# The cold start of a fused spectral-filter and feed-forward kernel: filters in three groups of loads, half of the forward table moved back, spare matmuls, a split last product

## The chip, the cores and the metric

One NeuronCore of one Trainium2 chip runs the whole program. The metric is device time in microseconds (us). Runs sent together share one chip and the same runs of the kernel before; runs sent at another time were on another chip, and I compare across those only through their ratios to the kernel before.

## The reference, cut to what matters

```python
X = np.fft.rfft(x, axis=1)                    # x: 8 batches, 3008 positions, 256 channels
F = (filt_r + 1j * filt_i)[None, :, :]
y = np.fft.irfft(X * F, n=3008, axis=1)       # then, with y as 24064 tokens of 256:
h = y @ w_in                                  # 256 -> 2048
out = (0.5 * h * (1.0 + erf(h / sqrt(2)))) @ w_out   # 2048 -> 256
```

## The kernel before

The Fourier transforms are matrix products with tables that the kernel computes itself. 3008 is factored as 47 x 64, which gives two forward steps (c1, c2), a product with the filters, and two backward steps (c3, c4), with transposes (c1t, c3t) between. Batches 1 to 7 are transformed beside the dense layers. **Batch 0 is not**: the dense layers cannot begin before it, so its whole chain stands in the open. That chain, and the tables and loads that it needs, are what the change rearranges. The parts concerned, with cuts:

```python
    def load_filters(self, k0, k):            # 4 loads on Pool's queue: real, imaginary, direct, mirror
        for t, src in enumerate((self.filt_r, self.filt_i)):
            ...
                nc.gpsimd.dma_start(out=self.F[32 * q:32 * q + 32, t, k0:k0 + k, :], in_=a)

    def dup_filters(self, eng, k0, k):        # partitions 0-63 copied to 64-127, two k at a time
        for k in range(k0, k0 + k, 2):
            o, i = (self.F[r:r + 64, :, k:k + 2, :].rearrange(...) for r in (64, 0))
            eng.tensor_copy(out=o, in_=i)

    def table_2_swap(self, h):                # half h of the forward table: rows swapped by PE, written by ACT
        t2 = self.T2[:, 12 * h:12 * h + 12]
        for s, j in ((1.0, 0), (-1.0, 32)):
            ps = self.bank("ps_sw", "n")
            self.nc.tensor.matmul(ps[:, 0:384], lhsT=self.swap, rhs=t2[:, :, 1, j:j + 32], ...)
            self._evac(t2[:, :, 2, j:j + 32], ps[:, 0:384].rearrange(...), "act", s)

    def table_2_minus(self, h):               # and its negative, by DVE
        self.nc.vector.tensor_scalar(out=t2[:, :, 0, :], in0=t2[:, :, 2, :], scalar1=-1.0, op0=ALU.mult, ...)
```

```python
    m.psum(wide, w=(2, 2), n=(4, 1))          # PSUM: two pairs of banks "w", four single banks "n"
    ...
    for k, n in ((0, 4), (4, 2), (6, 4), (10, 6), (16, 8)):
        m.load_filters(k, n)                  # 20 loads
    m.dup_filters(nc.gpsimd, 6, 4)
    m.load_w_in()
    ...
    m.dup_filters(nc.gpsimd, 10, 14)
    for u in range(16):
        m.c1(u // 2, u % 2, act if u < 4 or u % 2 else False)
        if u == 3:
            m.table_2_sin(0)
            m.table_2_swap(0)
        if u == 7:
            m.table_2_minus(0)
            m.table_2_sin(1)
            m.table_2_swap(1)
            m.table_2_minus(1)
        if u == 11:
            m.table_3(0, False)
    ...
    m.c1t(0, False)
    m.c1t(1, act)
    m.dup_filters(nc.vector, 0, 6)            # DVE copies the first six k itself
    for q in range(7):
        if q < 6:
            m.c2(2 * q)                       # products 2q and 2q+1: PE into a pair "w", DVE multiplies by F
            if q + 2 < 6:
                m.c1t(q + 2, act)
            m.c2(2 * q + 1)
        ...
        if q >= 1:
            m.c3(q - 1)
    ...
    m.psum(wide, v=(2, 2), t=(3, 1))
    for u in range(10):
        if u < 8:
            m.c3t(u)                          # transposes on PE, copied to d by DVE; u = 0 has a Pool memset of vt's end
        if u >= 2:
            m.c4(u - 2, False if u == 8 else act)   # both halves in one pair of banks, one evacuation
```

## Time and profile before

| before | us |
|---|---|
| time, median of 3 (later runs: 788.1 to 791.7) | 790.59 |
| span of the profiled run, whose time was 788.94 | 787.17 |
| first filter product starts | 22.54 |
| last filter product ends | 36.96 |
| first dense product starts | 46.67 |
| from there to the end | 740.50 |

The times inside the span are read from the timeline (start and duration of each row). The last row is PE-bound and untouched by the change.

### The profile page before, as it was taken

To read this page: it belongs to the slowest core of one execution; us is meant where nothing else is said; L and a number is where in the kernel's file an instruction comes from. 1 tells how busy PE (TensorE), PEld (TensorE's weight loads), DVE (VectorE), ACT (ScalarE), POOL (GpSimd) and SP (SyncE) were. 2 spreads that over 40 slices of the span, in tenths; PEclk is the share of its full clock that TensorE was granted. 3 is DMA by queue.
4 is the path that set the end of the run, shared out by engine and by line. 5 is a ranking of instruction groups with operands and counts; after the bars stand their busy time and mean duration, and the time that the engine had idled before them with its cause. 6 is when DMAs were issued, how large, how long until landed. Compare 5 with 4: busy or idle time off the path is not lost.

```text
span 787.2 us, 14592 instructions
## 1 busy us (share of the span) xinstructions
PE 762.2 (97%) x5821; PEld 540.1 (69%) x5918; DVE 406.7 (52%) x720; ACT 567.4 (72%) x968; POOL 65.7 (8%) x161
## 2 busy tenths in 40 slices
PE   4899999999999999999999999999999999999997
PEld 4766766677676767667677766667767677666666
DVE  6884756365563645546455564536645376411011
ACT  4788965788558975588755886568965788666663
POOL 8800200010000100001000110001100000000000
PEclk9999999999999999999999999999999999999999
DMA  8874753465334652447614465164642521510111
GB/s 130 151 135 139 140 148 79 144 123 113 106 101 141 115 146 74 108 131 139 146 40 123 138 126 149 49 172 92 130 121 73 157 80 56 134 37 32 41 41 55
DMA packets 86469, 85.64 MB, mean 109 GB/s; under 512 B 5888, under 2 KB 76608, under 8 KB 86400
## 3 DMA queue, kind: packets, MB, share of 16 engines
q1 hardware_dynamic: 77760, 68.70, 31.0%
q0 software_dynamic: 8640, 16.00, 14.3%
q8 instruction: 46, 0.75, 0.4%
q14 instruction: 23, 0.19, 0.1%
HBM read 54.00 MB, written 46.66 MB: 128 GB/s over the span
## 4 chain that ended last, share of the span: by engine, by line
PE 93%; DMA 3%; issue 1%; POOL 1%; ACT 1%; DVE 1%; SPq 0%; DVEq 0%; POOLq 0%
PE ps_o L450 42%; PE ps_h L436 38%; PE ps_s L253 3%; PE ps_s L326 3%; PE ps_s L276 2%; PE ps_s L301 2%; DMA d_sb<-R 1%; DMA x_sb<-in_x_dram 1%; ACT y_sb L238 1%; PE ps_c L380 1%; POOL F L91 1%; PE ps_c L364 1%; DMA b_sb<-R 0%; POOL x_sb L82 0%; DMA F<-in_filt_i_dram 0%
## 5 line engine op out<-in xcount | busy, mean ns | idle before, releaser
L439 ACT ACTIVATE g_sb<-ps_h 128x512 bf16<-128x512 f32 x752 | 439.4, 597 | 189.0 <-PE ps_h L436 162.0
L450 PE MATMUL ps_o<-w_out_sb,g_sb 128*128 128x256 bf16 x3008 | 449.1, 272 | 3.0
L436 PE MATMUL ps_h<-y_sb,w_in_sb 128*128 128x512 bf16 (+2 forms) x1503 | 426.6, 365 | 0.7 <-ACT y_sb L238 0.7
L450 PEld LDWEIGHTS <-g_sb 128*128 128x128 bf16 x3008 | 287.6, 98 | 133.7
L436 PEld LDWEIGHTS <-w_in_sb 128*128 128x128 bf16 x1600 | 155.0, 98 | 23.4 <-issue 0.9
L454 DVE COPY ost<-ps_o 128x512 f32<-128x512 f32 x94 | 64.4, 685 | 125.2 <-PE ps_o L450 124.7
L284 DVE TENSOR_TENSOR p<-ps_s,F 128x512 bf16<-128x512 f32 x84 | 58.1, 692 | 104.2 <-ACT p L283 97.6
L242 DVE TENSOR_SCALAR y_sb<-ps_s 128x376 bf16<-128x376 f32 x112 | 61.0, 548 | 81.6 <-PE ps_s L326 81.6
L240 DVE CAST a_sb<-ps_s 96x512 bf16<-96x512 f32 x112 | 76.3, 685 | 41.3 <-PE ps_s L253 41.3
L240 DVE CAST v_sb<-ps_s 128x512 bf16<-128x512 f32 x84 | 57.6, 687 | 12.9 <-PE ps_s L301 12.3
L282 ACT ACTIVATE p<-ps_s 64x512 bf16<-64x512 f32 x84 | 49.9, 594 | 2.4 <-PE ps_s L276 0.3
L326 PEld LDWEIGHTS <-d_sb 96*128 96x128 bf16 x448 | 30.4, 97 | 27.9 <-DMA d_sb<-R 2.6
L283 ACT CAST p<-ps_s 64x512 bf16<-64x512 f32 x84 | 48.5, 577 | 1.0
L101 POOL COPY gate<-p 1x1 bf16<-1x1 bf16 x48 | 8.5, 176 | 483.7 <-DVE p L286 483.7
L253 PE MATMUL ps_s<-x_sb,T 94*96 94x512 bf16 x112 | 42.6, 381 | 0.5
L326 PE MATMUL ps_s<-T,d_sb 96*128 96x94 bf16 x448 | 36.5, 204 | 2.0 <-DMA d_sb<-R 0.6
L286 DVE TENSOR_TENSOR p<-p 128x512 bf16<-128x512 bf16 x84 | 35.7, 425 | 2.9
L285 DVE TENSOR_TENSOR p<-p,F 128x512 bf16<-128x512 bf16 x84 | 34.9, 416 | 0.0
L82 POOL DMA_DIRECT2D x_sb<-in_x_dram x64 | 32.5, 510 | 13.3 <-issue 11.2
L276 PE MATMUL ps_s<-b_sb,T 128*128 128x256 bf16 x168 | 32.1, 273 | 0.8 <-DMA b_sb<-R 0.5
L301 PE MATMUL ps_s<-p,T 128*128 128x256 bf16 x168 | 32.1, 273 | 0.2
L301 PEld LDWEIGHTS <-T 128*128 128x128 bf16 x168 | 16.4, 98 | 20.1 <-DVE p L286 0.5
(94 smaller groups left out, 192.8 us busy)
## 6 DMA issues: line engine op xcount, KB each, us to landing
out_dram<-ost SPq DMA_DIRECT2D x94, 256.0 KB, 2.5
x_sb<-in_x_dram POOLq DMA_DIRECT2D x64, 188.0 KB, 3.9
R<-a_sb SPq DMA_DIRECT2D x56, 192.0 KB, 3.0
b_sb<-R SPq DMA_DIRECT2D x28, 384.0 KB, 4.3
R<-v_sb SPq DMA_DIRECT2D x42, 256.0 KB, 3.9
d_sb<-R SPq DMA_DIRECT2D x56, 192.0 KB, 4.7
w_in_sb<-in_moe_w_in_dram POOLq DMA_DIRECT2D x2, 512.0 KB, 6.3
w_out_sb<-in_moe_w_out_dram POOLq DMA_DIRECT2D x2, 512.0 KB, 10.7
```

What stands on the lines that cost most here:

```text
L240: self.nc.vector.tensor_copy(out=out, in_=in_)
L242: self.nc.vector.tensor_scalar(out=out, in0=in_, scalar1=scale, scalar2=None, op0=ALU.mult)
L253: nc.tensor.matmul(ps[0:96, :], lhsT=self.T1, rhs=self.st[b, "x"][:, 2 * u:2 * u + 2, :], start=True, stop=True)
L282: nc.scalar.activation(out=p2[0:64], in_=ps[64:128], func=AF.Copy, scale=-1.0)
L283: nc.scalar.copy(out=p2[64:128], in_=ps[0:64])
L284: nc.vector.tensor_tensor(out=p1, in0=ps, in1=f(0), op=ALU.mult)
L301: nc.tensor.matmul(ps[:, 256 * i:256 * i + 256], lhsT=self.T3[:, k].rearrange("p a b -> p (a b)"), rhs=w[:, 256 * i:256 * i + 256], start= ...
L326: nc.tensor.matmul(ps[:, 94 * i:94 * i + 94], lhsT=d[:, (grp % 2) * 4 + i, 128 * half:128 * half + 128], rhs=t4, start=True, stop=True)
L436: nc.tensor.matmul(ps[:, o:o + n], lhsT=self.w_in_sb[:, dc, jc * 128:jc * 128 + 128], rhs=self.ring[:, dc, off:off + n], start=(dc == 0), ...
L439: nc.scalar.activation(out=self.st["g", t][:, jc, :], in_=ps, func=AF.Gelu)
L450: nc.tensor.matmul(ps[:, tile_i % 2, :], lhsT=g[:, jc, tile_i * 128:tile_i * 128 + 128], rhs=self.w_out_sb[:, jc, :], start=(jc == 0), sto ...
L454: nc.vector.tensor_copy(out=ost, in_=ps)
```

## The change

The change means to bring the first dense product forward. It has five parts: (1) filters in three groups of loads (12 issues in place of 20), all copied by Pool; (2) the second half of the forward table (swap, minus), and table 3, moved from the middle of c1 to behind it, with the Gelu table load moved up; (3) the last product in two halves and c3 ordered by halves; (4) c3t ordered by halves, and c4 evacuated half by half out of five single banks; (5) ten spare matmuls while the input loads and three in c1, for PE's clock. The diff, with cuts (the new order of c3 is left out):

```diff
     def table_2_swap(self, h):
-        for s, j in ((1.0, 0), (-1.0, 32)):
-            ps = self.bank("ps_sw", "n")
-            ...
+        ps = self.bank("ps_sw", "w")
+        for i in range(2):
+            self.nc.tensor.matmul(ps[:, i, 0:384], lhsT=self.swap, rhs=t2[:, :, 1, 32 * i:32 * i + 32],
+                                  start=True, stop=True)
+        ...
+    def warm_up(self, n):
+        ps = self.bank("ps_warm", "n")
+        for i in range(n):
+            self.nc.tensor.matmul(ps, lhsT=self.ones[:, 0:128], rhs=self.ones, start=True, stop=True)
     def c2(self, p):
+        if p < 11:
+            nc.vector.tensor_tensor(out=w, in0=ps, in1=f.rearrange(...), op=ALU.mult)
+            return
+        for c in (slice(0, 128), slice(128, 256)):
+            nc.vector.tensor_tensor(out=w[:, :, :, c], in0=ps[:, :, :, c], in1=f[:, :, :, c], op=ALU.mult)
     def c3t(self, u):
-        for i in range(8):
+        for i in (0, 2, 4, 6, 1, 3, 5, 7):
     def c4(self, u, eng):
-        ps = self.bank("ps_c4", "v")
         for half in range(2):
+            ps = self.bank("ps_c4", "v")
             ...
-        self._evac(yv, ps[:, :, 0:376].rearrange(...), eng, 1.0 / self.S)
+            self._evac(yv, ps[:, 0:376].rearrange(...), eng[half], 1.0 / self.S)
 ...
+    m.ones = g.tile([128, 512], BF16, name="ones")
+    nc.vector.memset(m.ones, 1.0)
+    m.warm_up(10)
-    for k, n in ((0, 4), (4, 2), (6, 4), (10, 6), (16, 8)):
+    for k, n in ((0, 4), (4, 8), (12, 12)):
         m.load_filters(k, n)
-    m.dup_filters(nc.gpsimd, 6, 4)
     m.load_w_in()
-    m.dup_filters(nc.gpsimd, 10, 14)
+    m.dup_filters(nc.gpsimd, 0, K1)
     for u in range(16):
-        m.c1(u // 2, u % 2, act if u < 4 or u % 2 else False)
+        m.c1(u // 2, u % 2, act if u < 4 or u % 2 and u != 15 else False)
         if u == 3:
+            m.warm_up(3)
             m.table_2_sin(0)
+        if u == 7:
             m.table_2_swap(0)
-        if u == 7:
             m.table_2_minus(0)
+        if u == 11:
             m.table_2_sin(1)
-            m.table_2_swap(1)
-            m.table_2_minus(1)
-        if u == 11:
-            m.table_3(0, False)
+            nc.scalar.activation(out=warm, in_=m.p, func=AF.Gelu)
-    m.dup_filters(nc.vector, 0, 6)
     for q in range(7):
             m.c2(2 * q)
+            if q == 0:
+                m.table_2_swap(1)
             ...
-        if 1 <= q < 3:
+        if q == 1:
+            m.table_2_minus(1)
+        if q < 3:
             m.table_3(q, act)
 ...
-    m.psum(wide, v=(2, 2), t=(3, 1))
+    m.psum(wide, v=(5, 1), t=(3, 1))
```

More of the change, by code (lines that the diff above doesn't have):

```diff
@@ L191, in table_2_swap @@
         t2 = self.T2[:, 12 * h:12 * h + 12]
-        for s, j in ((1.0, 0), (-1.0, 32)):
-            ps = self.bank("ps_sw", "n")
-            self.nc.tensor.matmul(ps[:, 0:384], lhsT=self.swap, rhs=t2[:, :, 1, j:j + 32], start=True, stop=True)
-            self._evac(t2[:, :, 2, j:j + 32], ps[:, 0:384].rearrange("p (k j) -> p k j", k=12), "act", s)
+        ps = self.bank("ps_sw", "w")
+        for i in range(2):
+            self.nc.tensor.matmul(ps[:, i, 0:384], lhsT=self.swap, rhs=t2[:, :, 1, 32 * i:32 * i + 32],
+                                  start=True, stop=True)
+        for i in range(2):
+            self._evac(t2[:, :, 2, 32 * i:32 * i + 32], ps[:, i, 0:384].rearrange("p (k j) -> p k j", k=12),
+                       "act", 1.0 - 2.0 * i)
     def table_2_minus(self, h):
@@ L366, in c2 @@
                                  rhs=self.st[0, "b", k // 4][:, k % 4, :], start=True, stop=True)
-        nc.vector.tensor_tensor(out=w, in0=ps, op=ALU.mult,
-                                in1=self.F[:, :, 2 * p:2 * p + 2, :].rearrange("p t a b -> p t (a b)"))
+        f = self.F[:, :, 2 * p:2 * p + 2, :]
+        if p < 11:
+            nc.vector.tensor_tensor(out=w, in0=ps, in1=f.rearrange("p t a b -> p t (a b)"), op=ALU.mult)
+            return
+        w, ps = (v.rearrange("p t (a b) -> p t a b", a=2) for v in (w, ps))
+        for c in (slice(0, 128), slice(128, 256)):
+            nc.vector.tensor_tensor(out=w[:, :, :, c], in0=ps[:, :, :, c], in1=f[:, :, :, c], op=ALU.mult)
     def c3(self, q):
@@ L374, in c3 @@
         ps = [self.bank("ps_c3", "n") for half in range(2)]
-        for i in range(4):
+        for i, half in ((0, 0), (1, 0), (0, 1), (1, 1), (2, 0), (3, 0), (2, 1), (3, 1)):
             w = self.st[0, "p", 2 * q + i // 2]
-            for half in range(2):
-                o = 256 * (i % 2) + 128 * half
-                for t in range(2):
-                    self.nc.tensor.matmul(ps[half][:, 128 * i:128 * i + 128], lhsT=w[:, t, o:o + 128],
-                                          rhs=self.T3[:, 4 * q + i].rearrange("p a b -> p (a b)"),
-                                          start=t == 0, stop=t == 1)
+            o = 256 * (i % 2) + 128 * half
+            for t in range(2):
+                self.nc.tensor.matmul(ps[half][:, 128 * i:128 * i + 128], lhsT=w[:, t, o:o + 128],
+                                      rhs=self.T3[:, 4 * q + i].rearrange("p a b -> p (a b)"),
+                                      start=t == 0, stop=t == 1)
         for half in range(2):
@@ L409, in c4 @@
         d = self.st[0, "d", u // 2]
-        ps = self.bank("ps_c4", "v")
         for half in range(2):
+            ps = self.bank("ps_c4", "v")
             for i in range(4):
-                self.nc.tensor.matmul(ps[:, half, 94 * i:94 * i + 94],
+                self.nc.tensor.matmul(ps[:, 94 * i:94 * i + 94],
                                       lhsT=d[:, 4 * (u % 2) + i, 128 * half:128 * half + 128],
                                       rhs=self.T4c.rearrange("p a b -> p (a b)"), start=True, stop=True)
-        yv = self.ring[:, :, 0:self.S].rearrange("c h (m w) -> c h m w", w=HB)[:, :, :, 4 * u:4 * u + 4]
-        self._evac(yv, ps[:, :, 0:376].rearrange("c h (i m) -> c h m i", i=4), eng, 1.0 / self.S)
+            yv = self.ring[:, half, 0:self.S].rearrange("c (m w) -> c m w", w=HB)[:, :, 4 * u:4 * u + 4]
+            self._evac(yv, ps[:, 0:376].rearrange("c (i m) -> c m i", i=4), eng[half], 1.0 / self.S)
     def segs(self, t):
@@ L535 @@
             m.c2(2 * q + 1)
-        if 1 <= q < 3:
+        if q == 1:
+            m.table_2_minus(1)
+        if q < 3:
             m.table_3(q, act)
-        if q == 3:
-            nc.scalar.activation(out=warm, in_=m.p, func=AF.Gelu)
         if q >= 1:
@@ L551 @@
         if u >= 2:
-            m.c4(u - 2, False if u == 8 else act)
+            m.c4(u - 2, (act, False if u > 7 else act))
     wide.close()
```

## The prediction

> **What bounds the kernel now.** I read the page first. PE is 97% busy over a 787.2 us span, and its row of slices is full from the second slice on; only the first slice has room (PE 4 tenths, POOL 8).
>
> ```profile
> span 787.2 us, 14592 instructions
> PE   4899999999999999999999999999999999999997
> DVE  6884756365563645546455564536645376411011
> POOL 8800200010000100001000110001100000000000
> ```
>
> So the body is bound by PE and nothing in the diff touches it: every changed line belongs to the start, in which batch 0 is transformed before the first product of the dense layers. That product (L436) starts at 46.67 us. The question is how far it moves; all behind it moves along. The chain of waits narrowed to the start, then the timeline, show how the 46.67 us come about:
>
> ```profile
> 12.32 4.60 POOL F L91 x9
> 16.92 2.73 DMA F<-in_filt_i_dram
> 19.73 1.33 DVE F L96 x2
> ...
> 22.10 0.42 DVE F L96
> ```
>
> ```profile
> 19.68 2.21 POOL L96 COPY F<-F 64x1024 bf16<-64x1024 bf16 x2
> 19.73 2.78 DVE L96 COPY F<-F 64x1024 bf16<-64x1024 bf16 x3
> 22.54 4.62 DVE L367 TENSOR_TENSOR p<-ps_c,F 128x1024 bf16<-128x1024 f32 x4
> 23.82 6.93 POOL L96 COPY F<-F 64x1024 bf16<-64x1024 bf16 x7
> 27.82 9.14 DVE L367 TENSOR_TENSOR p<-ps_c,F 128x1024 bf16<-128x1024 f32 x8 [0.66 <-POOL F L96]
> 37.79 0.69 DVE L240 CAST vt_sb<-ps_c 128x512 bf16<-128x512 f32 x1 [0.83 <-PE ps_c L380]
> 39.24 5.56 DVE L240 COPY d_sb<-ps_c3t 96x1024 bf16<-96x1024 bf16 x8 [0.75 <-PE ps_c3t L399]
> 40.52 4.72 ACT L238 ACTIVATE y_sb<-ps_c 128x752 bf16<-128x752 f32 x6 [2.25 <-DVE d_sb L240]
> 45.30 0.49 PE L413 MATMUL ps_c<-T4c,d_sb 96*128 96x94 bf16 x8 [0.29 <-ACT y_sb L238]
> 45.83 0.80 ACT L238 ACTIVATE y_sb<-ps_c 128x752 bf16<-128x752 f32 x1 [0.58 <-PE ps_c L413]
> 46.67 0.38 PE L436 MATMUL ps_h<-y_sb,w_in_sb 128*128 128x512 bf16 x1 [0.67 <-ACT y_sb L238]
> ```
>
> The columns are start, duration of the row, engine, line, operation, count. Three stages follow one another. (1) Until 22.54: tables, c1, c1t, loading of the filters and their copying to the upper partitions. (2) 22.54 to 36.96: twelve filter products on DVE, 1.14 us apart, hardly interrupted. (3) 36.96 to 46.67: c3t and c4, where PE, ACT and DVE alternate.
>
> **What the skill says.** "SBUF — State Buffer", section "SBUF: two separate sides": DVE and GpSimd share one port pair under an exclusive lock, taken by a DVE operation in a two-port mode; the loser waits out the whole instruction. The trace agrees: the first two DVE copies of F start at 19.73 and 20.92, beside Pool's, and together end at 22.17 (about 1.25 us each), while the third, after Pool's pair, is 0.42. The products, with one input from PSUM, aren't held: they keep their 1.14 us beside Pool's copies. "TensorE: Matmul & The Clock Gate", Part 1: the array runs at half rate until about 3.4 us of sustained work, and falls back after an idle window. The trace agrees on the two rates: four 256-column products take 0.89 us at 21.41 and 0.44 at 24.95 (the chain's figure); the trace's first record of the full clock is at 22.0. "ScalarE: Activation LUTs", section "What ACT_TABLE_LOAD costs": an ACTIVATE with immediate scale takes 186 ns + 0.833 ns per element, back-to-back ones overlap by 93 ns, and a table load costs 1283 ns. Here 128x384 takes 493 (506 by the formula), 128x752 797 (812), the table load 1283.
>
> **Part 1, the filters: the start of stage 2.** Before, 20 Pool issues of about 0.53 us end at 19.64, and only then do copies begin. From the landing times in the trace: each Pool issue waits for the DMA eight before it; the last x load lands at 12.38 and the first four filter loads (0 to 3 in k) at 12.70 to 13.72. Until 13.3 Pool is held by these landings and the change can't hurry it. Behind that 4 issues remain in place of 12: 13.32 + 4 x 0.52 = 15.4. The two w_in issues (1.32, plus the two small T1 copies: 1.9 in all, as at 21.84 to 23.76) end at 17.3. They need the 5th and 6th filter load, now 128 KB each; I put those at 14.5 and 15.3, from 0.75 us for 128 KB (four such landed in 3.04 us between 21.46 and 24.50), so there is no wait. First copy: 17.36 + 1.04 = 18.4, then one each 0.98 us. Products can follow at 18.45 instead of 22.54. Pool's 0.98 outpaces DVE's 1.14, so the later copies stay ahead. The last filters, 4 x 192 KB behind about 17, land at some 21.5; copy 7 wants them at 23.3.
>
> **Part 2, the tables: does c2 arrive by 18.45?** Moving swap, minus and table 3 (DVE 1.23 us at 15.72) behind c1 removes what delayed c1's evacuations. ACT gains the Gelu table load behind the second sine (1.28 + 0.2, taken away from q = 3), and the last c1 tile goes to DVE. By hand: u = 8 waits for DVE at 11.4 as before (its angle chain ends at 10.91, unchanged), ACT does u = 9 and 11 until 12.65, sine until 13.5, load and warm until 15.0, u = 13 until 15.4; c1t(0) 15.45 to 16.0, DVE copy 0.69, c2(0) done 17.4. That is 1.1 us of slack behind Pool; at the half clock 0.3. So **Pool sets the start: 4.1 us earlier.**
>
> **Part 3, costs inside stage 2.** (a) swap(1) takes one of the two "w" bank pairs between c2(0) and c2(1), so c2(1) must wait for product 0: 1.14 becomes 1.22 + 0.65 (the matmuls and their latency) once, +0.7. (b) minus(1) lands on DVE between products 3 and 4 in a two-port mode: 0.35 alone, up to 1.3 behind a Pool copy, +0.85. (c) The last product in halves: 2 x 0.69 instead of 1.14, +0.2. (d) Before, 0.66 was lost at product 4, which I don't count on: -0.66 in the time after. Products: 18.45, 20.4, 21.55, 22.7, then 24.7 and on to 34.0, against 36.96: the 4.1 have shrunk to 3.0. I checked every c1t, table 3 and c3 of ACT and PE against this; ACT has about 0.8 us of slack.
>
> **Part 4, the end.** The halves let c3's first half go early, but ACT first evacuates c3(4) and table 4 (until about 34.65), so vt's half is ready at 35.25, and DVE's at 35.1: c3t begins 1.3 after the last product, before 1.6 (36.96 to 38.54). With even transposes first, the first d copy starts 0.5 to 0.6 later in place of 0.7, and is done at 36.6 against 39.93: 3.3. From there before took 6.7: six ACT evacuations paced by PE at 0.785 (PE's 0.45 + 0.33 per u), then c4(7), held for ACT's bank until 45.30 and evacuated alone, 0.8. After: 14 ACT halves at an estimated 186 + 313 - 93 = 406 ns from the ScalarE page (0.38 apart on the 128x384 of c1 here), started 0.25 sooner as half a c4 suffices; five banks take away the wait; c4(7)'s halves go to two engines, 0.5 each. DVE's eight copies (5.5) and two halves (1.05) end about as late. That is 6.0: 0.7 less. **mm1 at 42.65 instead of 46.67: 4.0 us.**
>
> **Part 5, spare matmuls.** Ten of 128x512 at the half clock are 4.3 us, from about 1.0 to 5.3, while PE waits for x until 5.95: free. They matter only if the clock stays up. In c1 afterwards PE would be working less than half the time and stands still from 12.9 to 15.4. A fall back to half rate before 20 us would add some 0.45 to c2(1) and 0.6 to c2(2), both now on the path: 1.0. I give it one in two: -0.5. It leaves **3.5 us**, 790.6 - 3.5 = 787.1.
>
> **Rivals.** *DVE simply follows Pool.* If Pool's copies are stretched to 1.2 us (as one of them was, 1.225 at 20.67), they pace the products: 12 x 1.2 from 17.4 ends at 31.8, still ahead of the last product at 32.6, so this costs nothing unless filters land over 2 us late; then perhaps 1 us: 788. *The halves make ACT the bound of c4:* 14 at 0.5 instead of 0.41 give back 1.2 us; the 0.38 of c1 speaks against it, the strided output for it: 788.2. *The time is hidden anyway:* mm1 would meet a late load. x of batch 1 lands from 34.4 to 41.6 and w_out at 44.2 and 47.4, and Pool issues them 1 us sooner; they are wanted from 42 and from 52: no. *All goes better:* clock up throughout, minus(1) lucky, 4.7 us: 785.9.
>
> **Range and chances.** The sum of known terms is 4.0; the clock term runs from 0 to 1, minus(1) by 0.5 either way, c4 by 1, the start by 0.7, and the three runs before spread 1.3. So 785.2 to 789.0. Two per cent would be 15.8 us, a third of the whole start: neither side is in reach.
>
> **What would show it.** First Pool copy of F at 17.4 and first product at 18.4 to 18.6, just behind it; a gap of 0.7 before the second and one of 0.4 to 1.3 before the fifth; last product ending near 34.0; no PE wait on ACT before the last c4; L436 starting near 42.7; the body unchanged. Were c2(0) rather than Pool the releaser of the first product, part 2 is wrong; were there holes in the products later, the slack of ACT in part 3. If mm1 starts 4 us earlier and the time doesn't move, the body isn't what I take it for.

## The result and the profile after

The changed kernel took 785.35 us (median of 4 runs, 785.00 to 786.51) against 790.00 (median of 4, 789.34 to 790.64) of the kernel before. The ratio is 0.9944, with a 95% interval of 0.9927 to 0.9961. Ratios here and below are the mean time of one kernel's runs over that of the other's of the same rounds, so they are not quite the ratio of the medians quoted. Within 2% is what was predicted; 785.35 lies in the range, near its lower edge. Sent a second time with the experiments (label a2_again), it gave 786.04 (6 runs, 785.45 to 786.94) and 0.9955 [0.9941, 0.9970], with 789.52 for the kernel before.

> The changed kernel once more, nothing edited. Its first profile had the first dense product at 43.70 us, 3.0 earlier than before, but its times are 4.4 us shorter, and it was the slowest of its four runs (786.5 against 785.0 to 785.4). Theory: the phase in which the half clock falls on the start differs from run to run (here it was at half rate from 12.43 to 19.25 us) and is worth about 1.2 us; then another profile shows other clock times, and where the full clock covers 16 to 20 us the second product starts near 19.9 instead of 21.1 and the first dense product near 42.5. Rival: the start is the same in every run and the spread arises in the body; then the first dense product is at 43.7 again, whatever the span. Time 785 to 786.5 under both.

In its profile the clock was half from 8.92 to 22.57 us, the second product started at 22.08 and the first dense product at 44.41. So the start does differ from run to run, here by 0.71 us, and the rival falls; a run of the change with the full clock from 16 to 20 us did not come up, so that half of the theory was left to e2.

The page of the changed kernel: the span, then three of its rows of 40 slices. PEclk is the clock that PE was granted, in tenths.

```profile
span 784.6 us, 14712 instructions
PE   6899999999999999999999999999999999999997
POOL 7801100010000100001000110001100000000000
PEclk8999999999999999999999999999999999999999
```

The first slice has more PE work in it (6 tenths for 4), and PE's clock in it is 8 tenths. The trace's clock record says when: full from 5.60 to 12.43 us, half from there to 19.25, then full to the end. In the kernel before it is full from 21.99 on. So the clock was awake early, **and then fell back in the stretch that matters**.

The chain of waits of the changed kernel, narrowed to its start (start, duration, what):

```profile
14.19 1.28 ACT L538
...
15.48 0.20 ACT warm L538
15.68 0.39 ACT at_sb L247
...
16.12 1.78 PE ps_c1t L361 x15
17.90 0.94 PE ps_c L373 x4
18.84 0.61 PE ps_sw L194 x2
...
19.47 0.88 ACT T L247 x2
...
20.39 0.61 PE ps_c L373 x4
...
21.10 1.24 DVE p L378
```

No Pool copy is in this chain. It runs through ACT's Gelu table load (L538, 1.28), the last c1 tile that waits behind it on ACT, the first transposes and the first c2 (both on PE at half clock: the four matmuls of c2(0) take 0.94 and those of c2(1) at full clock 0.61), and then through the swap, which PE writes and ACT evacuates, into the second c2.

The timeline of the changed kernel, with the rows that answer to those shown of before:

```profile
17.61 11.97 POOL L96 COPY F<-F 64x1024 bf16<-64x1024 bf16 x12
18.93 1.22 DVE L378 TENSOR_TENSOR p<-ps_c,F 128x1024 bf16<-128x1024 f32 x1 [1.16 <-DMA F<-in_filt_r_dram]
21.10 3.49 DVE L378 TENSOR_TENSOR p<-ps_c,F 128x1024 bf16<-128x1024 f32 x3 [0.94 <-PE ps_c L373]
24.50 1.24 DVE L202 TENSOR_SCALAR T<-T 128x768 bf16<-128x768 bf16 x1
25.66 8.00 DVE L378 TENSOR_TENSOR p<-ps_c,F 128x1024 bf16<-128x1024 f32 x7
33.58 1.28 DVE L382 TENSOR_TENSOR p<-ps_c,F 128x512 bf16<-128x512 f32 x2
36.84 5.55 DVE L249 COPY d_sb<-ps_c3t 96x1024 bf16<-96x1024 bf16 x8 [0.75 <-PE ps_c3t L412]
38.01 5.48 ACT L247 ACTIVATE y_sb<-ps_c 128x376 bf16<-128x376 f32 x14 [2.11 <-PE ps_c L426]
42.38 1.17 DVE L251 TENSOR_SCALAR y_sb<-ps_c 128x376 bf16<-128x376 f32 x2
43.70 0.59 PE L449 MATMUL ps_h<-y_sb,w_in_sb 128*128 128x512 bf16 x2 [0.52 <-DVE y_sb L251]
```

Pool's twelve copies run 0.98 apart (one, beside the minus, 1.11) and never hold a product back. The first product starts at 18.93. The row puts its wait down to a filter load, but that load had landed, and been copied, by 18.65; what ended last was c2(0), at 18.84 in the chain. A named releaser is to be checked against the time at which it was done.

Set beside each other, with the prediction's own figures (before its deduction for the clock):

| us | before | predicted | after | gained |
|---|---|---|---|---|
| first product starts | 22.54 | 18.45 | 18.93 | 3.61 |
| second product starts | 23.68 | 20.4 | 21.10 | 2.58 |
| fifth product starts | 27.82 | 24.7 | 25.66 | 2.16 |
| last product ends | 36.96 | 34.0 | 34.85 | 2.11 |
| c3t starts | 38.54 | 35.3 | 36.14 | 2.40 |
| first d copy done | 39.92 | 36.6 | 37.53 | 2.39 |
| first dense product | 46.67 | 42.65 | 43.70 | 2.97 |
| from there to the end | 740.50 | same | 740.89 | -0.39 |

The profiled pair thus shows 2.97 us at the dense layers and 2.6 in the span, less than the 4.45 by which the mean times differ. The profile of before comes from one of its faster runs (788.94) and that of after from the slowest of its four (786.51). And the remainder from the first dense product on varied between 739.1 and 741.4 us in the fourteen profiles, though no edit changes anything there. So **I read the start from the profiles and the worth of a kernel from the ratios**, and don't take a difference under 1 us in one span for an effect.

### The profile page after: what moved, and what is told of

Its sections match the earlier page's. It is cut to its first block, busy times and chain, and to the rows that moved or that the text cites. A ratio compares the mean times of both kernels' runs of the same rounds, so it can differ in the third digit from the quotient of the medians.

```text
span 784.6 us, 14712 instructions
## 1 busy us (share of the span) xinstructions
PE 769.8 (98%) x5931; PEld 538.9 (69%) x5931; DVE 404.5 (52%) x720; ACT 567.5 (72%) x975; POOL 64.2 (8%) x156
## 4 chain that ended last, share of the span: by engine, by line
PE 94%; DMA 3%; DVE 1%; ACT 1%; POOL 0%; issue 0%; SPq 0%; DVEq 0%; POOLq 0%
PE ps_o L463 41%; PE ps_h L449 40%; PE ps_s L262 3%; PE ps_s L335 3%; PE ps_s L310 2%; PE ps_s L285 2%; DMA d_sb<-R 2%; PE ps_c L373 1%; DMA x_sb<-in_x_dram 1%; PE ps_c L393 1%; PE ps_c3t L412 0%; DMA R<-v_sb 0%; POOL x_sb L82 0%; PE ps_c L426 0%; PE ps_c1t L361 0%
## 5 line engine op out<-in xcount | busy, mean ns | idle before, releaser
L449 PE MATMUL ps_h<-y_sb,w_in_sb 128*128 128x512 bf16 (+3 forms) x1600 | 447.6, 366 | 0.5 <-DVE y_sb L251 0.5
```

Source lines behind the costliest of these rows:

```text
L449: nc.tensor.matmul(ps[:, o:o + n], lhsT=self.w_in_sb[:, dc, jc * 128:jc * 128 + 128], rhs=self.ring[:, dc, off:off + n], start=(dc == 0), ...
```

## The experiments

Two theories stood at the outset. **Mine**: Pool sets the start, so the filter part brings the gain; the spares bring little, because the clock falls back. **The rival**: c2(0) sets the start, so the moved tables and the clock bring it. Two terms were disputed besides: the wait between the first two products and the minus on DVE. All results were correct against the reference, all verdicts are "same" (within 2%), and twelve kernels ran in three groups.

| run | ratio [95%] | median us | first product | last product ends | first dense product |
|---|---|---|---|---|---|
| the change, again | 0.9955 [0.9941, 0.9970] | 786.04 | 19.45 | 35.56 | 44.41 |
| e1 no spares | 0.9968 [0.9951, 0.9984] | 786.82 | 18.92 | 34.86 | 43.70 |
| e2 clock kept | 0.9946 [0.9932, 0.9961] | 785.38 | 18.85 | 34.04 | 42.89 |
| e4 swap in other banks | 0.9951 [0.9935, 0.9967] | 785.92 | 19.86 | 35.82 | 44.66 |
| e3 filters alone | 0.9971 [0.9954, 0.9988] | 787.63 | 20.85 | 35.86 | 45.58 |
| e8 tables alone | 0.9968 [0.9953, 0.9983] | 787.30 | 18.95 | 35.01 | 44.72 |
| e5 = e2, old c4 | 0.9945 [0.9923, 0.9967] | 784.87 | 18.66 | 33.17 | 42.59 |
| e7 = e2, minus on Pool | 0.9943 [0.9928, 0.9957] | 785.34 | 20.33 | 35.57 | 44.42 |
| e12 filters undone | 0.9941 [0.9929, 0.9953] | 785.07 | 19.06 | 34.95 | 43.80 |
| e13 spares alone | 0.9964 [0.9952, 0.9976] | 787.10 | 20.44 | 35.29 | 45.00 |
| e10 all repairs | 0.9944 [0.9927, 0.9961] | 784.88 | 17.86 | 32.42 | 44.35 |
| e11 = e10, minus on ACT | 0.9941 [0.9929, 0.9954] | 785.24 | 17.91 | 32.68 | 43.95 |

The four rows from "again" to e4 ran together (before: 789.52, 11 runs), then e3 to e7 (before: 789.75, 7 runs), then e12 to e11 (before: 789.92, 11 runs).

### e3, e8: the filter part alone, the table part alone

e3 is the kernel before with the three filter groups and Pool's copies; e8 is the kernel before with the moved tables only.

```diff
 e3, on the kernel before:
-    for k, n in ((0, 4), (4, 2), (6, 4), (10, 6), (16, 8)):
+    for k, n in ((0, 4), (4, 8), (12, 12)):
         m.load_filters(k, n)
-    m.dup_filters(nc.gpsimd, 6, 4)   ... and the other two dup_filters
+    m.dup_filters(nc.gpsimd, 0, K1)
 e8, on the kernel before: the hunks of table_2_swap, of the c1 loop, and of swap, minus, table_3 and Gelu in the q loop
```

> The kernel before with the filter part alone: three parts, all copied by Pool. Theory (in the kernel before the filters were only half of what held the first product: without DVE's copies it would still have waited for c2(0), ready at 20.76): first product at 20.8 instead of 22.54, second at 22.3 (c2(1) at half rate), last product ending near 34.9 instead of 36.96, first dense product 44.6 (46.67 before): 2.1 us earlier, some half of the whole gain. Rival (the filters are the gain, as my prediction's part 1 has it): first product at 18.5 to 19, first dense product near 43.7.

> The kernel before with the moved tables alone (swap, minus, table 3 and the Gelu load out of c1's way, swap in one bank pair). Theory: c2(0) is ready near 18.8 as in the changed kernel; DVE's three copies, now before Pool's begin at 19.7, cost 0.41 each instead of 1.25 and end near 19.0, so the first product starts at 19.0 and the second near 21.5 at half rate; first dense product 44.3, 2.3 us earlier. So either part alone brings over half of the gain, and the two don't add. Rival (Pool's copies after 19.7 are what holds the products): the first product still at 22 or later, or the fourth and sixth, which need Pool's copies of 20.7 and 24.85, late by over 1 us; first dense product 45.5 or later.

DVE's timeline of e3, the row of its first product:

```profile
20.85 1.23 DVE L367 TENSOR_TENSOR p<-ps_c,F 128x1024 bf16<-128x1024 f32 x1 [1.16 <-PE ps_c L364]
```

With the filters alone Pool's first copy was done by 19.00, and the product waited until 20.85 for c2(0), done at 20.76, exactly where it was in the kernel before. With the tables alone c2(0) was done at 18.83 and the product started at 18.95: as early as with the whole change, though DVE still made its three copies. By time, the filters alone are worth 1.95 us (means), the tables alone 2.47. Mine falls in its main point: **once DVE's copies are out of the way, c2(0) holds the start, and of these two parts only the tables move c2(0).** Which of the moves bundled in e8 does it was not separated, and the change with its table part alone undone was not run.

### e12: the whole change with the filters as they were

```diff
-    for k, n in ((0, 4), (4, 8), (12, 12)):
+    for k, n in ((0, 4), (4, 2), (6, 4), (10, 6), (16, 8)):
         m.load_filters(k, n)
+    m.dup_filters(nc.gpsimd, 6, 4)
-    m.dup_filters(nc.gpsimd, 0, K1)
+    m.dup_filters(nc.gpsimd, 10, 14)
+    m.dup_filters(nc.vector, 0, 6)
```

> The changed kernel with its filter part alone undone: five parts, copied by DVE and Pool as before. Theory (with the tables moved, the first product waits for c2(0), not for the filters: the run with the tables alone started it at 18.95 us against 18.93 in the changed kernel, at the same half clock): product 0 within 0.2 of c2(0)'s end, first dense product within 0.3 of the changed kernel at the same clock pattern (43.7 with the full clock from 19.2 on, 44.4 from 22.5 on), times 785.3 to 786.9, no measurable difference. Rival (the filter part is worth what my prediction's part 1 gave it): first product at 22, first dense product 46, about 3 us slower, 788.5 to 789.5.

The timelines of DVE and of Pool in e12, where the copies of F stand:

```profile
17.80 1.23 DVE L96 COPY F<-F 64x1024 bf16<-64x1024 bf16 x3
19.06 1.23 DVE L378 TENSOR_TENSOR p<-ps_c,F 128x1024 bf16<-128x1024 f32 x1
```

```profile
20.51 2.02 POOL L96 COPY F<-F 64x1024 bf16<-64x1024 bf16 x2
```

Undoing the filter part cost nothing: 0.9941 against 0.9944 and 0.9955, and the first dense product came at 43.80 against 43.70. The reason is on these rows. DVE's three copies now take 1.23 us together, because they are over before Pool's begin, and the first product follows them, 0.22 behind c2(0). In the kernel before, DVE's began at 19.73, 0.05 us after Pool's, and ended at 22.5: 2.78 us for 1.23. So what the prediction took for the price of the old filter part was a collision of copies, which goes away when the two sides start 1.2 us further apart. (This is shown at the half clock, which e12 had until 21.86; at the full clock the old filter part was not tried.) That also explains why the parts don't add: filters alone 1.95, tables alone 2.47, spares alone 2.79 us come to 7.2, and the whole brings about 4. An estimate: the collision's 1.55 us, counted three times instead of once, makes 3.1 of that excess. Each of them alone removes that one collision: e3 has no copies on DVE, in e8 DVE's are done at 18.92 before Pool's start at 19.83, in e13 at 20.41 before 20.57.

### e1, e13, e2: what the spare matmuls are worth

e1 is the change without spares, e13 the kernel before with the change's spares, e2 the change with 18 more spares spread over the rest of c1, to keep the clock up.

```diff
 e1, on the change:
-    m.warm_up(10)
-            m.warm_up(3)
 e13, on the kernel before:
+    m.warm_up(10)
+            m.warm_up(3)
 e2, on the change, in the c1 loop (fill writes to a pair "w"):
+        if u >= 4:
+            m.fill({7: 4, 11: 2, 15: 3}.get(u, 1))
```

> The changed kernel without its 13 spare matmuls. Theory (the full clock they bring at 5.6 us is lost again at 12.4, before the only stage that needs it, so they are worth next to nothing): within 0.5 us of the changed kernel, first dense product 43.3 to 44.3. Rival (they carry part of the gain): 1 us or more slower, 786.5 or above, with c1 itself later on the path and c1t(0) starting after 16.6 instead of 16.1.

> The kernel before with the 13 spare matmuls alone. In the changed kernel without them the mean was 0.98 us longer (787.09 against 786.11). Theory: in the kernel before they are worth little, because DVE's copies until 22.5 hold the first product however fast PE is, and only c2(1) and c2(2) at half rate come behind it: mean within 0.5 us of the kernel before (789.8), first dense product 46.2 to 46.9. Rival (the spread of the kernel before, 788.1 to 791.7, is the phase of the clock at 20 to 26 us): mean 0.8 to 1.5 shorter and the spread narrower.

> The changed kernel with 18 more spare matmuls between the c1 tiles, so that PE is hardly idle until c2 starts. Theory (half rate from 12.4 to 19.2 us costs 1.2 us by making c1t(0), c2(0), the swap and c2(1) late): the clock stays full from about 5.6 us on, product 0 starts at 18.7 behind Pool's first copy, product 1 at 19.9 to 20.1 in place of 21.1, first dense product 42.5, and the slower group of times (786.5) goes away: median 784.9. Rival 1 (the spare products get in the way of c1's own): c1t(0) starts later than 16.1 and nothing is gained. Rival 2 (the second product waits for ACT's swap evacuation whatever the clock): product 1 stays at 21.1.

Without spares the clock went up at 21.23 us. The means of e1 and of the change in the same rounds differ by 0.98 us, at the edge of what six runs each can tell; the one profile of e1 showed no loss at all (43.70, as in the change). On the kernel before the spares alone bring 0.9964, clearly more than nothing; in its profile the first product starts 2.10 us earlier (1.67 are left at the dense product), of which 0.44 are c2(0)'s (20.32 for 20.76) and the rest is the avoided collision; to that Pool contributed too, whose filter issues happened to end 0.9 later than in the profile of before. So my view that the spares bring next to nothing is wrong; how much of their worth is the clock itself stays open.

With the clock kept up (full from 4.43 us on) DVE's first two rows of products in e2 are:

```profile
18.85 1.23 DVE L383 TENSOR_TENSOR p<-ps_c,F 128x1024 bf16<-128x1024 f32 x1 [1.23 <-DMA F<-in_filt_r_dram]
20.26 3.49 DVE L383 TENSOR_TENSOR p<-ps_c,F 128x1024 bf16<-128x1024 f32 x3 [0.18 <-PE ps_c L378]
```

Now c2(0) is done at 18.27 and Pool's first copy at 18.82, and the product starts behind Pool, at 18.85. The wait before the second product shrinks from 0.94 to 0.18. The first dense product starts at 42.89, only 0.24 from the 42.65 that the prediction gave for a clock that holds. **With the clock kept the start is Pool's, as predicted; at the half clock, which the change in fact gets, it is PE's.** e5, which has the same start, agrees: c2(0) done at 17.83, Pool's first copy at 18.62, the product at 18.66. By time e2 is 0.71 us (means of the same rounds) better than the change, within the scatter.

### e4: does the swap's bank cause the wait of the second product?

The prediction has c2(1) wait for product 0, since swap takes one of the two pairs. In the program c2(1) got the pair that swap had used, so it waited for ACT's evacuation of the swap (19.47 to 20.35 in the chain above). e4 puts the swap into two single banks.

```diff
-        ps = self.bank("ps_sw", "w")
+        ps = [self.bank("ps_sw", "n") for i in range(2)]
```

> The changed kernel with the second half of the swap in two single banks, as before the change, so that c2(1) shares no bank with it. Theory (c2(1) waited from 20.2 to 20.39 and behind for ACT's evacuation of the swap at 19.47 to 20.35, the bank being the same): c2(1) runs at about 19.7 straight behind c1t(2), product 1 follows product 0 with no gap or 0.2 at most (20.1 to 20.4 instead of 21.1), first dense product 42.8 to 43.0 at the same clock pattern; 0.8 us faster, about 784.7. Rival (c2(1) waits for product 0, as my prediction had it, or PE is simply late at half rate): product 1 not before 20.9.

The wait stayed: 1.14 us before the second product. In this run the clock was full only from 5.76 to 9.18 and half until 22.83, and PE worked without a pause through c2(0), swap, c1t and c2(1) from 18.75 to 22.1. So with the bank freed, PE at half rate makes nearly the same wait: a2_again, half until 22.57 and with the shared bank, has 1.40, in which PE itself waited 0.11 for ACT. At the full clock and with the shared bank (e2, e5) PE waited 0.51 for ACT's evacuation, but the second product lost only 0.18 and nothing; in e10, with both repairs, the products 0 to 3 follow each other without a gap. So the half clock alone is enough for the wait, and the bank alone cost 0.18 at most. In the changed kernel, whose clock rose at 19.25, PE's wait for ACT is 0.51 of the 0.94; that pattern with the bank freed was not met in a profile.

### e5, e7: the split c4, and the minus

Both build on e2. e5 gives c4 back its pair of banks and its single evacuation; e7 moves the second minus to Pool, between the copies.

```diff
 e5:
-    m.psum(wide, v=(5, 1), t=(3, 1))
+    m.psum(wide, v=(2, 2), t=(3, 1))
-            m.c4(u - 2, (act, False if u > 7 else act))
+            m.c4(u - 2, False if u == 8 else act)      # and c4 itself as before
 e7:
-    m.dup_filters(nc.gpsimd, 0, K1)
+    m.dup_filters(nc.gpsimd, 0, 12)
-            m.table_2_minus(1)
+            m.table_2_minus(1, nc.gpsimd)
+            m.dup_filters(nc.gpsimd, 12, 12)           # and the later loads behind it
```

> The changed kernel with the spare matmuls through c1 (so that the clock is full in every run) and c4 as before: both halves in one bank pair, one evacuation of 752 elements. Theory: the time from the end of the first d copy to the first dense product, 6.17 us in the changed kernel and 6.74 in the kernel before, goes back to 6.7; first dense product 43.4 instead of 42.9, 0.5 us slower than the same kernel with split evacuations. Rival (the halves double ACT's fixed cost and give nothing): 6.2 or less stays.

> The changed kernel with the spare matmuls through c1 and the second minus on Pool, between its copies of filters 11 and 12, instead of on DVE between products 3 and 4, where it took 1.24 to 1.27 us (0.35 alone in c1) because of Pool's lock on the shared port. Loads of the next x and of w_out behind it. Theory: product 4 follows product 3 at once (0 to 0.2 instead of 1.1 us between them), first dense product 41.9 to 42.1 instead of 42.9; 0.7 to 0.9 us faster. Rival (product 4 is held by something else as well, as it was by 0.66 us in the kernel before and by 0.4 in the run without spare matmuls): half of that or less.

PE's timeline of e5, the last c4 and the first dense product:

```profile
41.22 0.49 PE L431 MATMUL ps_c<-T4c,d_sb 96*128 96x94 bf16 x8 [0.29 <-ACT y_sb L252]
...
42.59 0.38 PE L454 MATMUL ps_h<-y_sb,w_in_sb 128*128 128x512 bf16 x1 [0.67 <-ACT y_sb L252]
```

With the old c4 the two waits on ACT (0.29 and 0.67) are back, and the stretch from the first d copy to the dense product is 6.75 us again, for 6.17 with the halves. So the split is worth 0.58. That e5 still reached the dense product 0.30 earlier than e2 is due to its products: its minus came near the end of a Pool copy and not at its start (0.54 us for 1.27), and c1t began 0.43 earlier. Its times (784.34, 784.83, 784.92 and once 787.93) don't separate it from e2.

The rows of Pool and DVE in e7, around the minus:

```profile
23.79 2.14 POOL L202 TENSOR_SCALAR T<-T 128x768 bf16<-128x768 bf16 x1
```

```profile
25.97 2.35 DVE L383 TENSOR_TENSOR p<-ps_c,F 128x1024 bf16<-128x1024 f32 x2 [0.26 <-POOL T L202]
```

The fifth product then waits 0.26 us instead of being 1.2 late, but Pool needs 2.14 for what DVE does in 0.35 undisturbed. Nothing of it shows in the time (0.9943), and in this profile the start was lost elsewhere: the clock fell to half from 9.27 to 12.68 just where e2's fillers stand: from the fifth to the ninth c1 tile it took 4.16 us there for 2.53 in e2 (0.34 more came from an input load that landed later), and c1t began at 18.29 for 16.32. Spares that run at half rate were not free.

### e10, e11: all repairs in one kernel

e10 takes e2 with its swap in single banks (e4), the Gelu table load behind the products, six spares for three at u = 3, and Pool's filter copies ahead of the two w_in loads. e11 also makes the second minus on ACT.

```diff
 e10, on e2:
     m.load_filters(k, n)
+    m.dup_filters(nc.gpsimd, 0, K1)
     m.load_w_in()
-    m.dup_filters(nc.gpsimd, 0, K1)
-            m.warm_up(3)
+            m.warm_up(6)
-            nc.scalar.activation(out=warm, in_=m.p, func=AF.Gelu)      # at u == 11
+        if q == 4:
+            nc.scalar.activation(out=warm, in_=m.p, func=AF.Gelu)
 e11, on e10:
+        if h == 1: self.nc.scalar.activation(out=t2[:, :, 0, :], in_=t2[:, :, 2, :], func=AF.Copy, scale=-1.0); return
```

> A version that takes the found waits away: the changed kernel with spare matmuls through c1 (three more behind the first tiles), the swap in two single banks, the Gelu table load back in the products' stage (q = 4), where ACT has idle stretches of 1.2 us, and Pool's filter copies ahead of the w_in loads. Theory (at full clock what holds the first product is Pool's first copy at 18.6 to 18.8 and, behind it, c1t(0), which waits 0.9 us for ACT's last c1 tile behind the table load): c1t(0) at 15.4, Pool's first copy done at 16.9, c2(0) and product 0 at 17.4 to 17.7, product 1 straight behind; last product ends near 32.4, first dense product 41.2 (42.6 to 42.9 with the spare matmuls alone), time 783.8 to 784.2. Rival: the table load at q = 4 delays c3's evacuations and the products stall, or w_in, now loaded 12 us later, comes too late: first dense product 42.5 or later.

> The same with the second minus on ACT (one copy of 768 elements with scale -1, about 0.83 us) instead of on DVE, where Pool's lock stretched it to between 0.4 and 1.3. Theory: product 4 follows product 3 within 0.3 us; ACT's slack of about 0.8 us takes up most of its 0.83; first dense product 40.5 to 41.0, 0.3 to 0.7 earlier than the version with minus on DVE. Rival (ACT is too close to the bound in this stage, so c3's evacuations come late): no gain or a loss.

The products went as wanted. The first starts at 17.86, the last ends at 32.42 (e11: 32.68), 2.4 us earlier than in the change. But the first dense product came at 44.35 (e11: 43.95), later than the change's 43.70. The timeline of e10 between 39 and 42 us shows why:

```profile
39.92 0.89 POOL L115 DMA_DIRECT2D w_out_sb<-in_moe_w_out_dram  x1 [1.32 <-DMA x_sb<-in_x_dram]
40.80 0.17 POOL L410 MEMSET vt_sb<- 128x64 bf16 x1
...
41.02 0.72 PE L417 MATMUL ps_c3t<-eye,vt_sb 128*128 128x128 bf16 x5 [2.05 <-POOL vt_sb L410]
```

The memset of vt's end, which the last transposes need, is the last item in Pool's queue, behind the loads of the next batch and of w_out. I had moved w_in behind the filter copies, so it landed at 33.7 and 36.2, and every Pool issue waits for the load eight places ahead: the last x loads waited for w_in, w_out waited for x (which landed at 37.4 and 39.63), and the memset waited for w_out's issue. PE stood for 2.05 us (2.26 in e11). In the change the same memset is done at 35.6, before anyone wants it. In e10 PE's pause also cost the clock, which was half from 40.92 to 47.74, in the dense products themselves. This is the likely reason why e10 has four runs of 784.18 to 784.89 and two above 788, one of which is the profiled one; the mean clock of these two was 0.995 and 0.998, that of the four 0.999 or 1.0. Only the profiled one has a trace, so for the other the cause is argued, and even of the profiled run's excess about 1 us lies outside its span (788.66 against 785.7; in the four, 1.9 lie between time and span). The minus on ACT (e11) gained nothing: the fifth product starts 1.47 after the fourth in both, as e10's minus took only 0.35 on DVE.

So the gain of 2.4 us was real and was given back to a wait that the repair itself made. A kernel with the repairs of e10 and the memset ahead of the loads was not run, and no kernel that was run clearly beats the change.

## Why the prediction was right or wrong

**The size: right, but partly by luck.** 785.35 against 787.1 predicted, within 785.2 to 789.0. By e3, e8 and e12 the gain that part 1 gave to the filters came mainly from the tables, and two errors in size partly hide each other, see the last point.

**Part 1 and 2, "Pool sets the start: 4.1 us earlier": the step that failed.** The first product did come 3.61 us earlier, but not through Pool. The step put c2(0) at 17.4, 1.1 us ahead of Pool's first copy at 18.4; the copy was done at 18.65, c2(0) at 18.84. The 1.44 are: 0.67 because PE waited 0.58 for a bank that ACT had to free, so that ACT stood 0.76 between its two c1 tiles and its second sine began at 13.34, not 12.65 (the table load and the last tile behind it then followed in the predicted order); 0.41 for the first transposes and 0.36 for c2(0) with the hand-over, both at half clock. The prediction's "at the half clock 0.3" priced the clock rightly. Neither term alone, 0.67 or 0.77, would have put c2(0) behind Pool; the two together did.

What the old filter part cost was misread too. "Only then do copies begin", after Pool's last issue at 19.64, holds for Pool's copies. DVE's three, which the first product waited for, stood behind another row of DVE's timeline of the kernel before:

```profile
19.00 0.69 DVE L240 COPY b_sb<-ps_c1t 128x1024 bf16<-128x1024 bf16 x1 [1.13 <-PE ps_c1t L352]
```

They began at 19.73, straight behind this copy of the first transposes, though by the trace's landing times their filters had been there since 14.98. In e8, e12 and e13 too they begin 0.03 after it. So the table part, which brings the transposes forward, moves DVE's filter copies as well. e12 shows that the old filter part costs nothing once the copies of DVE and Pool no longer meet. I had seen the collision (1.25 us per copy) and cited the port lock for it, but treated it as the filter part's fixed price, not as an accident of 0.05 us that the table part would have removed as well.

**Part 3.** (a) The wait before the second product: 1.03 for 0.7, and by another mechanism: PE's half clock, and the swap's evacuation by ACT in place of product 0 (in e2 c2(1) started at 19.55, before product 0 ended at 20.08). By e4 the half clock is enough by itself; by e2 and e5 the bank alone cost 0.18 at most. (b) The minus: 1.24 us on DVE (0.85 expected, "up to 1.3" allowed), so the fifth product lost 1.16. e5's 0.54 and e8's 0.80 show that this is a matter of where Pool's copy stands; in both, as in the change, the minus ended 0.2 after a Pool copy did. (c) The halves: 1.28 for one of 1.22, so 0.05 and not 0.2. (d) The 0.66 of before is gone, as said. From first to last product the stage took 15.92 us; by the prediction 15.55.

**Part 4: right.** c3t began 1.29 after the last product (predicted 1.3), and from the first d copy on it was 6.17 for 6.75, 0.58 gained of 0.7; e5 confirms it by undoing it. ACT's 14 halves took 5.48, 0.39 each (predicted 0.406), so that rival falls. Only the first d copy's start, 0.70 after c3t in both kernels, did not move forward to 0.5 or 0.6 as I had said.

**Part 5: right in mechanism.** The clock came up at 5.60, fell at 12.43, and was half until 19.25: the fall-back that had been given even odds. (One reading of the two rates is off: the chain has 0.60 for the four matmuls at 24.95; its 0.44 stands at 26.88.) With the clock kept (e2) the dense product came 0.81 earlier, near the term of 1.0. It fell in all five profiled runs with just the change's spares, sometimes after one window only (a2_again: full from 5.50 to 8.92). So it was hardly a matter of one in two: the deduction of 0.5 should have been about 1.

**Where the gain came from.** By the runs, the tables alone are worth 2.47 us, the spares inside the change 0.98 (at the edge of the scatter), and the split c4 0.58 in the profiles: 4.0 together, near the whole's 3.67 and 4.45, with nothing left for the filters. As the parts need not add, this sum is an estimate.

**What the sum missed.** By the profiles the gain is 2.97, less than 3.5; by the times it is 4.45 (means) and, sent again, 3.67, more than 3.5. The prediction read all its waits from the profile of a run of 788.94 and subtracted from a median of 790.59. What made the usual run of before 0.6 to 1.7 us slower than the one profiled (medians of 789.52 to 790.59) was not in the reckoning, and the run of after that was profiled was its slowest. The collision at 19.7 and the instant at which the clock wakes are likely causes, as both depend on small shifts, but with one profile per kernel this is argued, not shown.

## What to carry to other kernels

When two engines are seen colliding in a profile, ask how far apart they started before booking the loss to one of the parts: a collision of copies that start 0.05 us apart disappears with any change that moves either side far enough (here 1.2 us), so such gains don't add, and a part should be tested both alone and by undoing it in the whole. When the array's clock is in doubt, work out the chain at both rates and see which step is last in each; here the last step changes from Pool to PE. And in a queue that issues loads in order, a tiny operation behind the loads (here a memset of 0.17 us) inherits all their waits, and a repair upstream can turn it into the bound.

## What the Trainium skill lacked or had wrong

- "TensorE: Matmul & The Clock Gate", Part 1, gives the window (3.41 us) and the two rates, and the trace agrees: all full and half stretches in the starts are 3.41, 6.83, 10.24 or 13.65 us long, and e10's one long full stretch, 34.13, is ten windows. It lacks how busy a window must be to keep the clock. Cut into these windows by the trace's clock record, PE was busy for 1.67 of the 3.41 us before the fall at 12.43, with no pause longer than 1.17, and for 2.04 of the window before, which kept the clock. In the seven profiles in which the clock fell in the start, the window before the fall had 1.47 (e10) to 1.91 (a2_again); windows that kept it had as little as 1.81 (the kernel before, from 21.99), 1.84 (e11) and 2.02 (e5). So in these runs the limit lies near a half of the window, and PE's busy time, whose ends are modelled, doesn't give it more closely: 1.81 kept the clock and 1.91 lost it. The page also has it that a ramp costs under 1% and isn't worth fitting; true here (about 1 us of 785), but in a change worth 0.5% it was one of the largest terms in doubt.
- "GPSIMD Engine Reference", section "4.1 Engine selection", has one-input operations on GpSimd "roughly line-rate". Here tensor_scalar on 128x768 bf16 took 2.14 us on Pool (e7) against 0.35 on DVE undisturbed (the first minus of the change, at 11.76), six times as long, though Pool copied 64x1024 in 1.03.
- No page that I read deals with the wait that a PSUM pair brings when it passes from one user to another: c2(1) got the pair that the swap had used, and PE waited 0.51 us for ACT to empty it (the change, e2, e5), but not in e10, where the swap has banks of its own.
- No page that I read says what an operation costs that is queued behind Pool's DMA issues: the memset in e10 was held until 40.80 by an issue that itself waited 1.32 us for another load, and PE lost 2.05 us.
